# The exponential's bias by two sums over neighbouring columns of one tile

## The chip, the cores and the metric

The kernel runs on one core of a Trainium2 chip. The metric is the device time of one execution in microseconds (us): the median of several runs, beside the time of one execution that was recorded by the hardware profiler.

## What is computed

Three layers follow one another: attention with random features (the part that the change is in), a dense layer with a sigmoid-gated unit, and a layer of eight experts of which each token takes one.

```python
def phi(x):                                   # x: q or k, scaled
    proj = np.einsum('bhsd,md->bhsm', x, omega)
    sq = np.sum(x * x, axis=-1, keepdims=True) / 2.0
    h = proj - sq
    h = h - np.max(h, axis=-1, keepdims=True)
    return np.exp(h) / np.sqrt(m)
q_p, k_p = (phi(q_s), phi(k_s))
kv = np.einsum('bhsm,bhsd->bhmd', k_p, v)
z = np.sum(k_p, axis=2)
num = np.einsum('bhsm,bhmd->bhsd', q_p, kv)
den = np.einsum('bhsm,bhm->bhs', q_p, z)[..., None] + 1e-06
out = num / den
...
g = h * (1.0 / (1.0 + np.exp(-1.702 * h)))    # h = x @ w_in
x = g @ w_out
...
ye = np.maximum(xe @ w1[e], 0.0) @ w2[e]      # e: the token's expert
```

Four batches, eight heads, 576 positions, head dimension 64 and 128 features make 2304 tokens of width 512.

## The kernel before

The tokens lie in 18 tiles of 128, each with all eight heads. The attention part goes over two sequences of tiles, k and q, with the k tiles five ahead (`LEAD`). First come the five k tiles alone. Then a loop over t does, as far as they exist: normalise q tile t-2 (`norm`), project k tile t+5 (`proj`), its bias and exponentials (`expo`), transpose the exponentials of q tile t-1 (`qtr`), add a k tile to the sums over keys (`ksums`), project q tile t, its bias and exponentials, then the numerator of q tile t-1 (`num`) and the transposed output of t-2 (`xtr`). From t = 13 on there are no k tiles left, and only q tiles are worked on. The order in the code is the order on every engine (`manual_schedule`); each engine runs its own instructions in order and waits on semaphores of the others.

For one tile the steps that matter are these. GpSimd squares the raw input (L219). TensorE sums the squares with a matmul against a column of `-0.5/sqrt(D)` (L227) into a corner of a PSUM bank; VectorE copies these sums for one k and one q tile into the SBUF tile `nsq` (L232, `sqkeep`). TensorE projects the tile into two PSUM banks `pj` (L256). VectorE takes the negated maximum over the 128 features of each of the eight heads, one instruction a bank (L263), into the SBUF tile `nm`, and then forms the bias in two operations of 128x8 elements: `nm - nsq` and then `nm + nsq` (L265, L266). The pair gives the same value as the negated maximum up to rounding: what is subtracted is the rounded `max + nsq`, as in the reference. ScalarE then takes the exponentials, eight instructions a tile, each with one column of `nm` as its bias (L269).

All PSUM banks of this part come from one pool of six (`work_bank`), so a step takes the banks that an earlier step of the sequence gave up: the numerator of one tile, with the norm sums in a corner of its first bank, takes the banks of the k projection, which are free when the k exponentials have read them.

Beside this, the dense layer's weights are converted, a chunk at a time: ScalarE takes an absolute value (L139), VectorE does four steps (L117, L118, L120, L122, handed out one by one by `cpop` behind `expo`), ScalarE rounds (L164) and GpSimd subtracts (L172, `clow`, and L179 for the activations' low halves). GpSimd's tensor_tensor instructions read both inputs from SBUF.

`nm` and `nsq` have three buffers each. An `nsq` buffer serves one k and one q tile.

Of the kernel before, what the change touches and what calls it, by code (L numbers as in the profile page):

```python
# [10 lines left out]
F32 = mybir.dt.float32  # L11
# [4 lines left out]
ALU = mybir.AluOpType  # L16
AX = mybir.AxisListType
# [53 lines left out]
def fused_kernel(ctx: ExitStack, tc: tile.TileContext, qT, kT, vt, omT, w_in, w_out, w_gate, w_gateT, w1, w2, consts, out):  # L71
    nc = tc.nc
# [115 lines left out]
    sp = sctx.enter_context(tc.tile_pool(name="atts", bufs=1, side="left"))  # L188
# [21 lines left out]
    sqs, nsq = {}, {}  # L210
# [16 lines left out]
                    nc.tensor.matmul(p[c:c + 64, 8 * i + j:8 * i + 8:4], s[:, j, c:c + 64], half, start=True, stop=True)  # L227

    def sqkeep(p, tiles):
        o = sp.tile([128, 2, 2, 4], F32, name="nsq", tag="nsq", bufs=3)  # L230
        n = len(tiles)
        nc.vector.tensor_copy(out=o[:, 0:n].rearrange("p a b c -> p (a b c)"), in_=p[:, 0:8 * n])  # L232
        for i, a in enumerate(tiles):
            nsq[a] = o[:, i]

    def sqfirst(tiles):
        p = work_bank("sq").rearrange("p a b -> p (a b)")
        sqsum(p, tiles)
        sqkeep(p, tiles)


    pj, phi = {}, {}
    kvps, kvsb = {}, {}

    def work_bank(name, w=128):
        return wkp.tile([128, 4, w], F32, name=name, tag="wk", bufs=6)
# [10 lines left out]

    def expo(kind, t):
        e = phi[kind, t] = (qp if kind == "q" else kp).tile([128, H, M], F32, name="phi" + kind, tag="phi" + kind, bufs=3)
        ps2, ns = pj.pop((kind, t)), nsq.pop((kind, t))  # L260
        nm = sp.tile([128, 2, 4], F32, name="nm", tag="nm", bufs=3)
        for g, p in enumerate(ps2):
            nc.vector.tensor_reduce(out=nm[:, g], in_=p, axis=AX.X, op=ALU.max, negate=True)  # L263

        nc.vector.tensor_tensor(out=nm, in0=nm, in1=ns, op=ALU.subtract)  # L265
        nc.vector.tensor_tensor(out=nm, in0=nm, in1=ns, op=ALU.add)  # L266
        for j in range(4):
            for g, p in enumerate(ps2):
                nc.scalar.activation(e[:, 2 * j + g], p[:, j], AF.Exp, bias=nm[:, g, j:j + 1])  # L269
# [62 lines left out]
    def norm(t):  # L332
        if t in rows:
            sqkeep(rows.pop(t), tiles(t + 2))
        dn = qp.tile([128, H], F32, name="dn", tag="dn", bufs=2)
        x = xns[t] = qp.tile([128, DM], F32, name="xn", tag="xn", bufs=2)
        for g, p in enumerate(nus[t]):
            nc.vector.tensor_scalar(out=dn[:, 4 * g:4 * g + 4], in0=p[:, :, D], scalar1=1e-6 * M, scalar2=None, op0=ALU.add)
        nc.vector.reciprocal(out=dn, in_=dn)
        for g, p in enumerate(nus.pop(t)):  # L340
            nc.vector.tensor_tensor(out=x[:, 256 * g:256 * g + 256].rearrange("p (h d) -> p h d", h=4), in0=p[:, :, 0:D],
                                    in1=bc(dn[:, 4 * g:4 * g + 4], D, 2), op=ALU.mult)
# [26 lines left out]
    for i in range(WARM):  # L369
        p = work_bank("wm")  # L370
# [54 lines left out]
    for t in range(LEAD):  # L425
        proj("k", t)
        sqfirst([("k", t)])
        expo("k", t)
        if t >= 1:
            ksums(t - 1)  # L430
        advance()
        if t >= LEAD - 2:
            cload(1)
    for t in range(NT):
# [5 lines left out]
        if k < NT:  # L440
            proj("k", k)
            expo("k", k)
            advance()
# [5 lines left out]
        if k == NT:  # L449
            kctx.close()  # L450
            xa = ctx.enter_context(tc.tile_pool(name="xa", bufs=1, side="right"))
            php = ctx.enter_context(tc.tile_pool(name="ph", bufs=1, space=PSUM, side="right"))
        proj("q", t)
        expo("q", t)
        cstore()
        cabs(1)
# [280 lines left out]
    for n in range(len(steps) + 1):  # L737
        if n < len(steps):
            b, f = steps[n]
# [51 lines left out]
            if (b, f) == (0, HF):  # L791
                assert cnext[4] == len(order)
                for i in range(2):
                    wg.append(keep.tile([128, 4, DM], F32, name=f"wg{i}", tag=f"wg{i}", bufs=1))
                    nc.sync.dma_start(out=wg[i].rearrange("p e d -> p (e d)"),
                                      in_=w_gate[4 * i:4 * i + 4].rearrange("(o e) d -> o (e d)", o=1).to_broadcast([128, 4 * DM]))
# [23 lines left out]
        if n < len(steps):  # L820
# [9 lines left out]
            if wg and (b, f) not in pfirst:  # L830
                room = BUDGET[b]
                while pend and room > 0:
                    a = pend.pop(0)
# [301 lines left out]
```

## Time and profile before

| what | value |
|---|---|
| runs: median (lowest to highest) | 839.61 us (837.99 to 841.62), 3 runs |
| the profiled execution | 842.98 us |
| its span, first to last instruction | 841.1 us |
| TensorE busy | 793.1 us, 94% |
| VectorE busy | 490.0 us, 58% |
| ScalarE busy | 372.5 us, 44% |
| GpSimd busy | 127.0 us, 15% |

Times in the profile are in us from the start of the span, those of single instructions partly in ns. PE is TensorE (PEld its weight loads), DVE VectorE, ACT ScalarE, POOL GpSimd, SP the queue that issues the transfers. L265 is line 265 of the kernel. A row such as `nm<-nm,nsq 128x8` says what is written from what, with the partitions and elements. In brackets stands how long the engine was idle before the instruction and what released it; where several things were waited for, the one that came last by the profile is named, and it can have been another. "issue" is idle time for which the profile shows no wait. The granted clock (PEclk) is 1.00 at TensorE's full 2.4 GHz and 0.50 at 1.2 GHz. A busy TensorE is not necessarily one at its peak, since matmuls are pipelined.

### The profile page before, as it was taken

Reading aid. Unit: us, or ns where it says so; the run is one execution under the profiler, and the core shown is the slowest. Engines: PE = TensorE matmul, PEld = TensorE weight load, DVE = VectorE, ACT = ScalarE, POOL = GpSimd, SP = SyncE. Lnnn points to the kernel's source line nnn. Section 1 sums busy time; section 2 is a strip of 40 time slices with the busy share of each in tenths; the row PEclk is TensorE's granted clock in tenths of the full one; section 3 lists DMA queues with packets and bytes.
Section 4 is the critical chain, followed back from the end, with each engine's and each line's share of the span. In section 5 each row is a group of like instructions: output and inputs, shape, how many; then the busy total and the mean of one; then the engine's idle time right before and its main releaser. Section 6 shows DMA issues by size and latency. Waiting matters only on the chain.

```text
span 841.1 us, 17414 instructions
## 1 busy us (share of the span) xinstructions
PE 793.1 (94%) x6833; PEld 704.6 (84%) x6833; DVE 490.0 (58%) x1170; ACT 372.5 (44%) x873; POOL 127.0 (15%) x131
## 2 busy tenths in 40 slices
PE   9888888977999999999999999999999999999994
PEld 7777777755878888888888988998999999999993
DVE  3566565666986631786631775473488565556551
ACT  4666666774554433122222222222444655555551
POOL 2332222220000001010001001200014312201111
PEclk9988888998999999999999999999999999999998
DMA  8633443335888646444333644796227656555101
GB/s 219 189 101 115 116 115 102 114 101 175 289 303 272 190 157 217 130 149 149 95 94 88 183 128 122 223 344 206 88 66 293 210 204 223 182 182 185 30 29 32
DMA packets 68410, 134.74 MB, mean 160 GB/s; under 512 B 24800, under 2 KB 24928, under 8 KB 63968
## 3 DMA queue, kind: packets, MB, share of 16 engines
q1 hardware_dynamic: 65088, 124.04, 46.2%
q0 software_dynamic: 3072, 9.44, 3.8%
q8 instruction: 56, 0.92, 0.5%
q14 instruction: 34, 0.28, 0.1%
q10 hardware_dynamic: 160, 0.07, 0.0%
HBM read 118.84 MB, written 18.87 MB: 164 GB/s over the span
## 4 chain that ended last, share of the span: by engine, by line
PE 58%; issue 25%; POOL 7%; DVE 6%; ACT 2%; DMA 1%; POOLq 0%; SPq 0%; ACTq 0%; DVEq 0%
PE py L511 7%; PE py L512 7%; PE py L514 7%; PE ph L485 7%; PE ph L486 7%; PE ph L487 7%; PE pj L256 4%; POOL out L894 2%; PE tr L312 2%; PE kv L286 2%; POOL yg L679 2%; PE nu L227 2%; PE nu L330 2%; DVE nm L263 1%; POOL sq L219 1%
## 5 line engine op out<-in xcount | busy, mean ns | idle before, releaser
L500 ACT ACTIVATE gh<-ph 128x512 fp32r<-128x512 f32 (+1 forms) x80 | 44.5, 556 | 233.2 <-PE ph L487 233.2
L502 DVE TENSOR_TENSOR gl<-sg,gh 128x512 fp32r<-128x512 f32 (+1 forms) x80 | 51.1, 639 | 161.1 <-ACT sg L501 160.9
L487 PE MATMUL ph<-xh,l 128*128 128x512 f32 (+1 forms) x320 | 118.0, 369 | 1.6 <-DMA l<-lod 1.6
L485 PE MATMUL ph<-xh,win 128*128 128x512 f32 (+1 forms) x320 | 118.8, 371 | 0.0
L486 PE MATMUL ph<-xl,win 128*128 128x512 f32 (+1 forms) x320 | 117.8, 368 | 0.3 <-DVE xl L179 0.3
L511 PE MATMUL py<-wo,gh 128*128 128x512 f32 x288 | 113.6, 394 | 4.6 <-ACT big L348 4.6
L512 PE MATMUL py<-l,gh 128*128 128x512 f32 x288 | 113.5, 394 | 0.0
L546 DVE CUSTOM_DVE_ANT_0 junk<-ysb,wg 128x512 f32<-128x512 f32 x120 | 87.0, 725 | 3.1
L514 PE MATMUL py<-wo,gl 128*128 128x512 f32 x288 | 79.3, 393 | 0.0
L179 POOL TENSOR_TENSOR xl<-big,xh 128x512 fp32r<-128x512 f32 (+1 forms) x20 | 24.2, 1210 | 328.5 <-PE py L512 168.4
L851 PE MATMUL ph<-yhl,wh 128*128 128x288 f32 x256 | 71.8, 303 | 0.0
L867 PE MATMUL oT<-gh,wh 128*128 128x288 f32 x256 | 71.2, 301 | 0.0
L852 PE MATMUL ph<-yhl,wh 128*128 128x288 f32 x256 | 69.9, 295 | 0.0
L868 PE MATMUL oT<-gh,l 128*128 128x288 f32 x256 | 69.3, 294 | 0.0
L487 PEld LDWEIGHTS ph<-xh,l 128*128 128x128 f32 x320 | 60.0, 188 | 9.5 <-DMA l<-lod 2.0
L486 PEld LDWEIGHTS ph<-xl,win 128*128 128x128 f32 x320 | 60.1, 188 | 9.1 <-DVE xl L179 0.7
L511 PEld LDWEIGHTS py<-wo,gh 128*128 128x128 f32 x288 | 54.5, 189 | 15.4 <-ACT big L348 4.9
L485 PEld LDWEIGHTS ph<-xh,win 128*128 128x128 f32 x320 | 60.2, 188 | 8.6
L263 DVE TENSOR_REDUCE nm<-pj 128x4 f32<-128x512 f32 x72 | 46.3, 684 | 34.0 <-PE pj L256 31.2
L514 PEld LDWEIGHTS py<-wo,gl 128*128 128x128 f32 x288 | 54.7, 190 | 11.9
L512 PEld LDWEIGHTS py<-l,gh 128*128 128x128 f32 x288 | 54.7, 190 | 10.4
L179 DVE TENSOR_TENSOR l<-f,wh 128x512 fp32r<-128x512 f32 x64 | 46.3, 751 | 27.3 <-ACT wh L178 27.1
(187 smaller groups left out, 1492.5 us busy)
## 6 DMA issues: line engine op xcount, KB each, us to landing
l<-lod SPq DMA_DIRECT2D x160, 256.0 KB, 3.1
f<-w SPq DMA_DIRECT2D x20, 1024.0 KB, 6.1
e<-w SPq DMA_DIRECT2D x16, 1024.0 KB, 5.3
st<-w_in SPq DMA_DIRECT2D x16, 512.0 KB, 5.0
st<-w_out SPq DMA_DIRECT2D x16, 512.0 KB, 5.0
lod<-l SPq DMA_DIRECT2D x32, 256.0 KB, 2.1
yd<-ysb SPq DMA_DIRECT2D x22, 256.0 KB, 2.5
raw<-kT SPq DMA_DIRECT2D x18, 256.0 KB, 2.8
```

Source lines behind the costliest of these rows:

```text
L179: eng.tensor_tensor(out=lo, in0=src, in1=hi.bitcast(F32), op=ALU.subtract)
L485: nc.tensor.matmul(p, wh[:, c], xh, start=k == 0, stop=False)
L486: nc.tensor.matmul(p, wh[:, c], xl, start=False, stop=False)
L487: nc.tensor.matmul(p, wl[:, c], xh, start=False, stop=k == KC - 1)
L511: nc.tensor.matmul(p, gh[:, c], wh, start=(b, f) in pfirst, stop=False)
L512: nc.tensor.matmul(p, gh[:, c], wl, start=False, stop=False)
L514: nc.tensor.matmul(p, gl[:, j * 128:(j + 1) * 128], wh, start=False, stop=(b, f) in plast)
L546: nc.vector.tensor_tensor_reduce(out=junk, in0=ysb[b][j], in1=wg[e // 4][:, e % 4], scale=1.0, scalar=0.0, op0=ALU.mult, op1=ALU.add, accu ...
L851: nc.tensor.matmul(p, wh[:, w], yh[:, k], start=k == 0, stop=False)
L852: nc.tensor.matmul(p, wh[:, w], yl[:, k], start=False, stop=False)
L867: nc.tensor.matmul(p, wh[:, w], hh, start=f == 0, stop=False)
L868: nc.tensor.matmul(p, wl[:, w], hh, start=False, stop=False)
```

## The change

The tile `nsq` gets three columns for each of the eight heads: the maximum (column 0), the sum of squares (column 1), and a scratch value (column 2). The copy of the sums of squares writes column 1. The maxima are no longer negated and go to column 0. The first of the two operations becomes a negated sum over columns 0 and 1, written to column 2; the second a sum over columns 1 and 2, written to `nm`. The values are the same. Line numbers below these lines go up by one.

```diff
--- before.py
+++ after.py
@@ -227,9 +227,10 @@
                     nc.tensor.matmul(p[c:c + 64, 8 * i + j:8 * i + 8:4], s[:, j, c:c + 64], half, start=True, stop=True)
 
     def sqkeep(p, tiles):
-        o = sp.tile([128, 2, 2, 4], F32, name="nsq", tag="nsq", bufs=3)
+
+        o = sp.tile([128, 2, 8, 3], F32, name="nsq", tag="nsq", bufs=3)
         n = len(tiles)
-        nc.vector.tensor_copy(out=o[:, 0:n].rearrange("p a b c -> p (a b c)"), in_=p[:, 0:8 * n])
+        nc.vector.tensor_copy(out=o[:, 0:n, :, 1].rearrange("p a b -> p (a b)"), in_=p[:, 0:8 * n])
         for i, a in enumerate(tiles):
             nsq[a] = o[:, i]
 
@@ -257,13 +258,13 @@
 
     def expo(kind, t):
         e = phi[kind, t] = (qp if kind == "q" else kp).tile([128, H, M], F32, name="phi" + kind, tag="phi" + kind, bufs=3)
-        ps2, ns = pj.pop((kind, t)), nsq.pop((kind, t))
+        ps2, o = pj.pop((kind, t)), nsq.pop((kind, t))
         nm = sp.tile([128, 2, 4], F32, name="nm", tag="nm", bufs=3)
         for g, p in enumerate(ps2):
-            nc.vector.tensor_reduce(out=nm[:, g], in_=p, axis=AX.X, op=ALU.max, negate=True)
-
-        nc.vector.tensor_tensor(out=nm, in0=nm, in1=ns, op=ALU.subtract)
-        nc.vector.tensor_tensor(out=nm, in0=nm, in1=ns, op=ALU.add)
+            nc.vector.tensor_reduce(out=o[:, 4 * g:4 * g + 4, 0], in_=p, axis=AX.X, op=ALU.max)
+
+        nc.vector.tensor_reduce(out=o[:, :, 2], in_=o[:, :, 0:2], axis=AX.X, op=ALU.add, negate=True)
+        nc.vector.tensor_reduce(out=nm.rearrange("p a b -> p (a b)"), in_=o[:, :, 1:3], axis=AX.X, op=ALU.add)
         for j in range(4):
             for g, p in enumerate(ps2):
                 nc.scalar.activation(e[:, 2 * j + g], p[:, j], AF.Exp, bias=nm[:, g, j:j + 1])
```

The sequence of instructions stays on every engine; what changes on VectorE is the operations and what they wait for. Here are VectorE's rows in the attention loop for one k tile, before (in brackets the engine whose semaphore is waited for; `nm` is the bias, `nsq` the sums of squares, `pj` the projection, `cf` a weight chunk, `dn` and `xn` the normalised output):

```order
L341 TENSOR_TENSOR xn<-nu,dn 128x256
L263 TENSOR_REDUCE nm<-pj 128x4 [waits PE_49,Activation_49]
L263 TENSOR_REDUCE nm<-pj 128x4 [waits PE_49]
L265 TENSOR_TENSOR nm<-nm,nsq 128x8 [waits DVE_49]
L266 TENSOR_TENSOR nm<-nm,nsq 128x8 [waits DVE_49]
L122 SCALAR_TENSOR_TENSOR cf<-st_111,cf 128x512
```

and in the changed kernel at the same place:

```order
L342 TENSOR_TENSOR xn<-nu,dn 128x256
L264 TENSOR_REDUCE nsq<-pj 128x4 [waits PE_49] x2
L266 TENSOR_REDUCE nsq<-nsq 128x8 [waits DVE_49]
L267 TENSOR_REDUCE nm<-nsq 128x8 [waits DVE_49,Activation_49]
L122 SCALAR_TENSOR_TENSOR cf<-st_111,cf 128x512
```

The wait on ScalarE, for the exponentials that last read this buffer of `nm`, stands at the second sum now instead of the first maximum. The rows before and behind are the same instructions as before.

## Rows read from the trace of the kernel before

**Rows 1.** Busy time by stretch: stretch; us; busy us by engine; granted clock; DMA; GB/s.
```profile
40.00:152.00 112.00, 95.54 (x1950) 83.42 (x1952) 70.79 (x180) 71.29 (x226) 29.33 (x27) 0.83 0.40 111
```

**Rows 2.** Operations on the tile nm: count; ns min/median/max; first and last start.
```profile
L265 DVE TENSOR_TENSOR nm<-nm,nsq x36: 166/168/1283, 9.6 to 182.3; 128x8 f32<-128x8 f32 x36
```

**Rows 3.** Order of time, 73.9 to 81.4 us: start, us, engine, line, operation, idle before.
```profile
73.99 1.27 POOL L172 TENSOR_TENSOR l<-cf,win 128x512 fp32r<-128x512 f32 x1 [4.11 <-ACT win L164]
74.01 1.26 DVE L265 TENSOR_TENSOR nm<-nm,nsq 128x8 f32<-128x8 f32 x1
75.21 1.04 POOL L219 TENSOR_TENSOR sq<-raw 128x512 f32<-128x512 f32 x1
75.31 0.96 DVE L266 TENSOR_TENSOR nm<-nm,nsq 128x8 f32<-128x8 f32 x1
76.20 0.41 DVE L118 TENSOR_SCALAR cf<-cf 128x512 int32<-128x512 int32 x1
76.37 2.18 ACT L269 ACTIVATE phik<-pj,nm 128x128 f32<-128x128 f32 x8 [2.46 <-DVE nm L266]
...
79.55 2.04 POOL L219 TENSOR_TENSOR sq<-raw 128x512 f32<-128x512 f32 x2 [3.29 <-PE nu L227]
81.27 0.17 DVE L232 COPY nsq<-nu 128x16 f32<-128x16 f32 x1 [2.46 <-PE nu L330]
```

**Rows 4.** Order of time, TensorE: the norm sums at L227, 39 to 109 us.
```profile
39.92 1.10 PE L227 MATMUL nu<-half,sq 128*64 128x2 f32 x32 [1.19 <-issue]
...
48.48 1.10 PE L227 MATMUL nu<-half,sq 128*64 128x2 f32 x32 [0.74 <-issue]
...
57.65 1.66 PE L227 MATMUL nu<-half,sq 128*64 128x2 f32 x32 [1.69 <-POOL sq L219]
...
68.06 1.10 PE L227 MATMUL nu<-half,sq 128*64 128x2 f32 x32 [0.45 <-issue]
...
78.39 1.88 PE L227 MATMUL nu<-half,sq 128*64 128x2 f32 x32 [2.66 <-issue]
...
89.03 1.10 PE L227 MATMUL nu<-half,sq 128*64 128x2 f32 x32 [0.69 <-issue]
...
98.47 1.54 PE L227 MATMUL nu<-half,sq 128*64 128x2 f32 x32 [2.08 <-issue]
...
108.77 1.10 PE L227 MATMUL nu<-half,sq 128*64 128x2 f32 x32 [0.33 <-issue]
```

**Rows 5.** Busy time by stretch: the microsecond from 41 us.
```profile
41.00:42.00 1.00, 1.00 (x23) 1.00 (x23) 0.07 (x1) 1.00 (x6) 1.00 (x2) 0.50 0.08 23
```

**Rows 6.** Busy time by stretch, VectorE on tile nsq (L265, L266): busy; clock; DMA.
```profile
26.00:27.20 1.20, 1.05 (x2) 1.00 0.77 280
53.90:55.55 1.65, 1.31 (x2) 1.00 0.73 230
69.00:70.15 1.15, 1.01 (x2) 1.00 1.01 353
73.90:76.30 2.40, 2.23 (x2) 1.00 0.78 212
94.50:96.40 1.90, 1.65 (x2) 1.00 0.81 199
...
158.00:159.50 1.50, 1.16 (x2) 1.00 0.48 171
169.80:171.80 2.00, 1.84 (x2) 1.00 0.00 0
182.20:184.22 2.02, 1.83 (x2) 1.00 0.00 0
```

**Rows 7.** Operations on the tile om, at 614 us.
```profile
L953 DVE TENSOR_TENSOR om<-oh,start x1: 301/301/301, 614.5 to 614.5; 128x144 f32<-128x144 bf16 x1
L954 DVE TENSOR_REDUCE pgt<-om x1: 303/303/303, 614.8 to 614.8; 128x18 f32<-128x144 f32 x1
```

**Rows 8.** Groups of instructions from 40 to 152 us: the maxima.
```profile
L263 DVE TENSOR_REDUCE nm<-pj 128x4 f32<-128x512 f32 x45 | 29.0, 684 | 22.5 <-PE pj L256 22.5
```

## Prediction

> **What bounds the kernel now.** I read the busy time by stretch first, then the operations on the bias tile, the order of time around one slow tile, and last TensorE's idleness along the attention part. The first two show where a change in this code can act: L265 runs from 9.6 to 182.3 us of the span [rows 2], so what is saved there moves the rest forward as it stands; and from 40 to 152 us TensorE's granted clock is 0.83 on average [rows 1].
>
> The two operations that the change removes should be equal small pieces of work, 128x8 elements each, and most are: the median of L265 is 168 ns, but the longest of the 36 took 1283 [rows 2], and L266 is like it. Time order shows why. At 74.01 us L265 starts beside GpSimd's subtract (L172, at 73.99 for 1.27 us) and lasts 1.26 us; L266 starts at 75.31 beside GpSimd's square (at 75.21 for 1.04 us) and lasts 0.96 us: each ends as the GpSimd instruction ends [rows 3]. The small copy at 81.27, whose input lies in PSUM, takes its usual 0.17 us inside the two squares of 79.55 to 81.59 [rows 3]. So a VectorE operation with two SBUF inputs waits for a GpSimd tensor_tensor that is running; one that reads PSUM alone does not.
>
> This wait is on the path. ScalarE's eight exponentials of the k tile start only behind L266 (76.37, for 2.18 us [rows 3]), and TensorE's next step (the norm sums, L227, and the numerator) needs the PSUM bank that the seventh of them frees: it starts at 78.39, after 2.66 us of idleness [rows 4]. I call an interval from one start of L227 to the next *heavy* where GpSimd's L172 falls on the k tile's bias (every second one: a weight chunk is converted over two tiles), else *light*. TensorE idles 1.69, 2.66 and 2.08 us at the end of the first three heavy intervals, and 0.74, 0.45, 0.69 and 0.33 us at the end of light ones [rows 4].
>
> After long idleness TensorE is slow. The 32 norm sums take 1.10 us behind gaps of 0.33 to 0.74, and 1.66, 1.88 and 1.54 us behind the long ones [rows 4]. Behind the gap of 1.19 at 39.92 too the clock fell: from 41 to 42 us it is 0.50, the 1.2 GHz level [rows 4, 5]. So a late bias is paid twice, as idleness and as a light interval at half clock.
>
> **The change, part by part.** *What goes.* Per tile (36 tiles) L265 and L266, with whatever wait each has. Rows 6 give the two together where they met GpSimd; 2 x 0.168 = 0.34 us of it is work [rows 2, 6].
> (a) Heavy k tiles: 1.31 - 0.34 = 0.97, then 1.89 and 1.31 us [rows 6], and two later ones (115 and 136 us) like the second: 8.0 us. Each is smaller than the TensorE gap behind it (1.69, 2.66, 2.08 [rows 4]), so all of it comes off the path: 8.0.
> (b) The q-only tiles at the end (from 152 us): 0.82, 1.50 and 1.49 us [rows 6]. There is no other tile to work on there: projection, maxima, bias, exponentials and transposes follow one another. I take the first two whole. In the third the chain also runs through the conversion step behind L266, which has two SBUF inputs and would meet the same GpSimd pair. Between 0 and 1.49 I take 1.2, because an operation that waited slipped in between two GpSimd instructions (L265 ended at 75.27, the square had begun at 75.21 [rows 3]). Together 3.5.
> (c) The start: 1.05 - 0.34 = 0.7 at 26 us [rows 6], bounded by 0 if the loads set the pace there; taken as 0.7.
> (d) Four q tiles among the k tiles, the costliest being of the kind of the 0.67 us at 69 us [rows 6]. Their exponentials have until the transposes, and the normalisation behind them waits for the numerator anyhow; 0.4 for all, between 0 and 4 x 0.67 = 2.7.
>
> *What comes.* Two tensor_reduce of 128x16 to 128x8 per tile. The trace has no such size; the nearest pair is a tensor_tensor on 128x144 at 301 ns and, right behind it, a tensor_reduce of 128x144 into 18 groups at 303 ns [rows 7]: groups cost nothing to speak of. Eight elements more than now are 8/144 of what of the 303 ns grows with size, at most 17 ns. Between 0 and 17 ns an operation, on some 24 tiles of the path (18 k, the last q), the far end is 0.8 us; I take 0.3. The Trainium skill speaks against the change here: "VectorE: DVE Perf Modes", section "Rules for kernel authors", calls tensor_reduce the slowest VectorE operation, to be restructured on a hot path. Its one element a cycle at 0.96 GHz makes the eight elements 8 ns, an estimate: 0.4 us on those tiles in place of my 0.3. By the rows of 301 and 303 ns the reduce is no slower than what it replaces.
>
> *What is only rearranged.* The maxima lose their sign flip and write every third element, as does the copy; both still read PSUM. The wait for the exponentials of three tiles back moves from the first maximum to the second sum, which is later and so can only be over sooner. I cost these at nothing: VectorE waits 22.5 us for projections before the 45 maxima from 40 to 152 us [rows 8]; without that cover, 10 ns more on each of 72 maxima would be 0.7 us.
>
> *What is late next.* TensorE then waits for maxima, two short sums and seven exponentials. The gaps become 1.69 - 0.97 = 0.72, 2.66 - 1.89 = 0.77 and 2.08 - 1.31 = 0.77 us. They lie by 0.74, after which the clock stayed, and below 1.19, after which it fell.
>
> (e) The clock. Heavy intervals without the wait are (57.65 - 48.48) - 0.97 = 8.20, 10.33 - 1.89 = 8.44 and 9.44 - 1.31 = 8.13 us; the light ones at half clock are 10.41, 10.64 and 10.30 [rows 4]. A light interval at full clock should then be about 8.3, so a stretch at half clock that vanishes gives 2.1 us. Five of them follow heavy tiles: 0 if none vanishes, 10.5 for all. With gaps so near 0.74 I take three: 6.3.
>
> Sum: 8.0 + 3.5 + 0.7 + 0.4 - 0.3 + 6.3 = 18.6 us. The profiled execution took 842.98 us (1.88 more than its span) and becomes 824.4. It lies 3.37 us above the median of the runs (839.61), so the forecast for the median is **821.0 us**.
>
> **The rivals.**
> *A, the clock keeps falling.* The waits go, but gaps of 0.7 us, now at the end of every interval, bring half clock as often as before: 12.3 us of gain, 827.3 us. For it: one gap of 1.19 was enough. Against: four gaps of 0.33 to 0.74 passed [rows 4].
> *B, the clock stays up* in all five: 12.3 + 10.5, so 816.8 us. The same rows speak for it.
> *C, the wait is inherited.* Behind L266 stands one step of the weight conversion (L118, at 76.20 for 0.41 [rows 3]). It now comes up while GpSimd still works. If it is held to the end of the square (76.25), VectorE is free at 76.66 instead of 76.61: the k exponentials are early all the same, and lost are (d), the 1.2 of (b) and 0.05 in five tiles: 1.9 us, 822.9 us. The Trainium skill, "SBUF — State Buffer", section "Who interferes with whom", lists tensor_scalar in its two-port mode among what contends with GpSimd, so by it L117 and L118 could be held like the two-input steps.
> *D, the change doesn't do what it says.* The sums read SBUF, and the copy at 81.27 shows only that a PSUM input escapes [rows 3]. If one SBUF input waits as well, all stays: 839.61 + 0.3 = 839.9 us. The same section of the Trainium skill says that tensor_reduce never contends on trn2; no run here shows it yet.
> *E, slower.* From 1.19 us of idleness in every interval on, half clock would be the rule: heavy intervals grow by 2.1 each (5 x 2.1 - 8.0 = +2.5), the five q-only tiles, now at 1.00 [rows 6], likewise (10.5 - 3.5 = +7.0), less (c) and (d), 1.1, and with the 0.3: 848.3 us. Against it: behind a light interval at half clock the gap is small (0.45, 0.69, 0.33 [rows 4]), so a slow TensorE closes its own gaps.
>
> **How the numbers follow.** Forecast 0.43, A 0.21, B 0.17, C 0.10, D 0.06, E 0.03. A measurement of this kernel can tell about 0.5% (4.2 us) from no change. Forecast, A, B and C are all faster by more: 0.91; D is no change: 0.06; E is slower: 0.03. The range reaches down to B with 2.1 more of (d) and the 1.6 us by which a run lay below the median: 813. Up it reaches to A without (c), without the 1.2 of (b), and with the 2 us by which a run lay above: 831.
>
> **What would show it.** In the profile after, both sums should last about 0.17 us in every tile, beside GpSimd too; if their longest is above 0.5 us, D holds. TensorE's idleness before L227 stays below 1.2 us, and the granted clock from 40 us to the end of the k tiles rises from 0.83 to about 0.93; at 0.83 it is A, at 1.00 B. The stretches behind the attention part keep their lengths. The prediction is wrong if the attention part shortens by under 8 us or by over 27.

## The result and the profile after

The changed kernel takes 817.61 us in the median of four runs (813.85 to 817.84) where the kernel before, on the same chip, takes 838.80 (836.17 to 841.62): a ratio of 0.9736, with a 95% interval from 0.9693 to 0.9780. The forecast was 821.0 in a range of 813 to 831; rival B, that the clock stays up behind all five heavy tiles, gave 816.8. The measurement lies at B.

| | before | after |
|---|---|---|
| the profiled execution | 842.98 us | 817.50 us |
| its span | 841.1 us | 815.7 us |
| TensorE's granted clock, mean of the span | 0.969 | 0.990 |

**The two sums.** The tile view of `nsq` in the changed kernel shows (count; ns min/median/max; first and last start):

```profile
L266 DVE TENSOR_REDUCE nsq<-nsq x36: 169/170/171, 9.6 to 159.7; 128x8 f32<-128x16 f32 x36
L267 DVE TENSOR_REDUCE nm<-nsq x36: 169/170/171, 9.8 to 160.0; 128x8 f32<-128x16 f32 x36
```

Where [rows 2] had a longest of 1283 ns, and the second operation one of 1191,

```profile
L266 DVE TENSOR_TENSOR nm<-nm,nsq x36: 166/166/1191, 10.0 to 183.0; 128x8 f32<-128x8 f32 x36
```

the longest of the 72 is now 171. By the medians one sum costs 2 to 4 ns more than the operation it replaces.

**TensorE's gaps and its clock.** TensorE's norm sums of the changed kernel in order of time (start, us, engine, line, operation, in brackets the idleness before), the counterpart of [rows 4]:

```profile
39.09 1.10 PE L227 MATMUL nu<-half,sq 128*64 128x2 f32 x32 [1.19 <-issue]
...
47.14 1.10 PE L227 MATMUL nu<-half,sq 128*64 128x2 f32 x32 [0.23 <-issue]
...
55.25 1.10 PE L227 MATMUL nu<-half,sq 128*64 128x2 f32 x32 [0.72 <-POOL sq L219]
...
63.69 1.10 PE L227 MATMUL nu<-half,sq 128*64 128x2 f32 x32 [0.77 <-issue]
...
71.85 1.10 PE L227 MATMUL nu<-half,sq 128*64 128x2 f32 x32 [0.77 <-POOL sq L219]
...
80.28 1.10 PE L227 MATMUL nu<-half,sq 128*64 128x2 f32 x32 [0.77 <-issue]
...
88.45 1.10 PE L227 MATMUL nu<-half,sq 128*64 128x2 f32 x32 [0.78 <-POOL sq L219]
```

and by stretch (stretch; us; busy us by engine with instructions; granted clock; DMA; GB/s):

```profile
41.00:44.00 3.00, 3.00 (x43) 2.55 (x40) 1.82 (x6) 1.85 (x7) 1.15 (x2) 0.50 0.00 0
45.00:150.00 105.00, 93.36 (x2173) 78.80 (x2169) 77.28 (x205) 82.76 (x258) 34.52 (x31) 1.00 0.45 132
```

The gaps of 1.69, 2.66 and 2.08 us at the end of the first three heavy intervals became 0.72, 0.77 and 0.78 (at 55.25, 71.85 and 88.45), as worked out. The norm sums take 1.10 us behind every one of them. In this execution half clock is left in one place of the k tiles, behind the gap of 1.19 at 39 us, which no heavy tile makes and which was there before [rows 4, 5]. From 45 to 150 us the granted clock is 1.00, the 2.4 GHz level; before, it was 0.83 from 40 to 152 us [rows 1].

It is not so in every execution. A second profiled one of the same kernel (`change_again`, experiment 6) has a gap of 0.93 us at 104 us, as this one has at 105.04; there the numerator behind it takes 1.92 us, here 1.16:

```profile
104.24 1.10 PE L227 MATMUL nu<-half,sq 128*64 128x2 f32 x32 [0.93 <-POOL sq L219]
105.16 1.92 PE L331 MATMUL nu<-kvsb,qTs 128*64 128x65 f32 x32
```

Its clock is 0.66 from 106 to 110 us, and that interval takes 9.40 us instead of 8.67.

**The wait has not gone, it has moved.** The tile view of a weight chunk `cf` in the kernel before, the three conversion steps that VectorE runs behind the bias:

```profile
L117 DVE TENSOR_SCALAR cf<-cf x32: 413/422/429, 35.7 to 294.3; 128x512 f32<-128x512 f32 x32
L118 DVE TENSOR_SCALAR cf<-cf x32: 412/427/429, 37.7 to 294.7; 128x512 int32<-128x512 int32 x32
L120 DVE SCALAR_TENSOR_TENSOR cf<-st,cf x32: 678/691/815, 40.4 to 295.2; 128x512 int32<-128x512 int32 x32
```

and in the changed kernel:

```profile
L117 DVE TENSOR_SCALAR cf<-cf x32: 416/421/1135, 34.8 to 269.3; 128x512 f32<-128x512 f32 x32
L118 DVE TENSOR_SCALAR cf<-cf x32: 415/428/1246, 36.9 to 269.8; 128x512 int32<-128x512 int32 x32
L120 DVE SCALAR_TENSOR_TENSOR cf<-st,cf x32: 680/693/1427, 39.6 to 270.3; 128x512 int32<-128x512 int32 x32
```

Time order around the heavy tile at 69 us of the changed kernel, the counterpart of [rows 3], shows who holds whom:

```profile
69.07 1.27 POOL L172 TENSOR_TENSOR l<-cf,win 128x512 fp32r<-128x512 f32 x1 [3.57 <-ACT win L164]
69.30 0.17 DVE L266 TENSOR_REDUCE nsq<-nsq 128x8 f32<-128x16 f32 x1
69.57 0.17 DVE L267 TENSOR_REDUCE nm<-nsq 128x8 f32<-128x16 f32 x1
69.66 0.97 DVE L118 TENSOR_SCALAR cf<-cf 128x512 int32<-128x512 int32 x1
69.83 2.18 ACT L270 ACTIVATE phik<-pj,nm 128x128 f32<-128x128 f32 x8 [0.84 <-DVE nm L267]
...
70.30 1.22 POOL L219 TENSOR_TENSOR sq<-raw 128x512 f32<-128x512 f32 x1
...
72.62 1.04 POOL L219 TENSOR_TENSOR sq<-raw 128x512 f32<-128x512 f32 x1 [1.10 <-PE nu L227]
72.73 0.17 DVE L267 TENSOR_REDUCE nm<-nsq 128x8 f32<-128x16 f32 x1
...
72.82 1.39 DVE L120 SCALAR_TENSOR_TENSOR cf<-st,cf 128x512 int32<-128x512 int32 x1
...
75.27 1.10 PE L257 MATMUL pj<-omx,raw 64*64 64x128 f32 x30 [0.39 <-DVE xn L342]
```

Both sums run inside GpSimd's L172 at their usual length, and ScalarE's exponentials start at 69.83, before L172 ends. The conversion step L118 behind them is held: 0.97 us instead of 0.43, past the end of L172 at 70.34. At 72.82 L120 is held too, 1.39 instead of 0.69. From 40 to 140 us the 19 steps of L117, L118 and L120 take 9.3 us more than at the medians of before (by the groups of instructions: 7 of L120 at a mean of 1265 ns, 6 of L118 at 924, 6 of L117 at 802). In heavy tiles this lies beside the exponentials and costs nothing. In the light interval (from 71.85) it does not: VectorE comes late to the normalisation `xn`, and TensorE waits 0.39 us for it. The chain of work that ended last, of the changed kernel from 69 to 76 us (start, us, what), passes through it:

```profile
70.05 1.10 PE pj L257 x32
71.15 1.28 DVE nsq L264 x2
...
72.90 1.31 DVE cf L120
...
74.70 0.43 DVE xn L342
...
75.27 0.73 PE pj L257 x17
```

**Where the 25.4 us between the two spans lie.** From the norm sums at 39 us (TensorE in order of time) to the numerator that follows the last stretch at half clock of before, L330 at 151.59, and the same one after, L331 at 131.12: 151.59 - 39.92 = 111.67 and 131.12 - 39.09 = 92.03, so 19.6. From there to the dense layer's first product `py` (199.67 and 175.76): 48.08 and 44.64, so 3.4. Behind it 641.4 and 639.9: 1.5. And 0.8 ahead of the first. The profiled execution of before was itself 3.4 us above the median of the three runs that were known then, the one of after lies at its median; so of the 25.4, some 22 are the change (839.61 - 817.61; with the fourth run of before, 838.80 - 817.61 = 21.2).

The 19.6 can be split by the intervals between the norm sums (L227, to 150.90 before and 130.44 after). The first interval is 0.5 us shorter. The five heavy ones took 49.6 us together and now take 40.9: 8.7, of which the waits by term (a) are 8.0. The five light ones behind them took 52.8 and now take 42.4: 10.4. No wait of the bias lies in the light ones; what they had is half clock.

### The profile page after: what moved, and what is told of

It reads as the page before. It is cut to its first block, busy times and chain, and to the rows that moved or that the text cites. A ratio compares the mean times of both kernels' runs of the same rounds, so it can differ in the third digit from the quotient of the medians.

```text
span 815.7 us, 17416 instructions
## 1 busy us (share of the span) xinstructions
PE 778.5 (95%) x6833; PEld 691.5 (85%) x6833; DVE 483.6 (59%) x1170; ACT 371.9 (46%) x873; POOL 128.8 (16%) x131
## 4 chain that ended last, share of the span: by engine, by line
PE 58%; issue 24%; DVE 9%; POOL 6%; ACT 2%; DMA 1%; POOLq 0%; ACTq 0%; SPq 0%; DVEq 0%
PE py L512 8%; PE py L513 8%; PE py L515 7%; PE ph L486 7%; PE ph L487 7%; PE ph L488 7%; PE pj L257 5%; PE kv L287 3%; POOL out L895 2%; POOL yg L680 2%; DVE nsq L264 2%; PE tr L313 2%; DVE cf L120 1%; PE nu L331 1%; POOL G L1003 1%
## 5 line engine op out<-in xcount | busy, mean ns | idle before, releaser
L264 DVE TENSOR_REDUCE nsq<-pj 128x4 f32<-128x512 f32 x72 | 46.4, 686 | 29.1 <-PE pj L257 29.1
L513 PEld LDWEIGHTS py<-l,gh 128*128 128x128 f32 x288 | 54.7, 190 | 10.4
```

The costliest lines, as they stand in the source:

```text
L513: nc.tensor.matmul(p, gh[:, c], wl, start=False, stop=False)
```

## The experiments

The theory: a GpSimd instruction on SBUF holds a VectorE operation with two SBUF inputs, the sums, each a tensor_reduce with one input, pass, and TensorE gains twice, in idleness and in clock. The rivals: that the new tile's columns or the moved wait give the gain; that the clock has no part in it; that the sums' own length is all that counts. Each kernel was run beside the kernel before on the same chip (medians of before: 838.92, 838.27 and 838.58 us in the three groups). Where an experiment adds lines, its line numbers are shifted by them.

**1. The new tile with the old operations.** All of the change but the operation:

```diff
-        nc.vector.tensor_reduce(out=o[:, :, 2], in_=o[:, :, 0:2], axis=AX.X, op=ALU.add, negate=True)
-        nc.vector.tensor_reduce(out=nm.rearrange("p a b -> p (a b)"), in_=o[:, :, 1:3], axis=AX.X, op=ALU.add)
+        nc.vector.tensor_tensor(out=o[:, :, 2], in0=o[:, :, 0], in1=o[:, :, 1], op=ALU.subtract)
+        nc.vector.tensor_tensor(out=nm.rearrange("p a b -> p (a b)"), in0=o[:, :, 2], in1=o[:, :, 1], op=ALU.add)
```

with the maxima negated as before.

> The changed kernel's tile with three columns, its strided maxima and copy and its moved semaphore waits, but the bias formed by two tensor_tensor (two SBUF inputs each) as before. Port theory (a tensor_tensor with two SBUF inputs waits for a running GpSimd tensor_tensor): the waits return, longest of either operation about 1.2 us, granted clock from 40 to 140 us back near 0.83, time as before, 837 to 842 us. Rival, the tile's layout or the moved waits made the gain: about 818 us, both operations at 0.17 us.

Measured: 831.29 us (827.95 to 833.54), ratio 0.9914 [0.9875, 0.9952]. The waits are back, as the tile view and time order show:

```profile
L266 DVE TENSOR_TENSOR nsq<-nsq x36: 170/172/1056, 9.5 to 172.9; 128x8 f32<-128x8 f32 x36
L267 DVE TENSOR_TENSOR nm<-nsq x36: 168/170/1186, 9.7 to 173.9; 128x8 f32<-128x8 f32 x36
```

```profile
71.70 0.17 DVE L266 TENSOR_TENSOR nsq<-nsq 128x8 f32<-128x8 f32 x1
71.76 1.27 POOL L172 TENSOR_TENSOR l<-cf,win 128x512 fp32r<-128x512 f32 x1 [3.93 <-ACT win L164]
71.98 1.07 DVE L267 TENSOR_TENSOR nm<-nsq 128x8 f32<-128x8 f32 x1
...
75.16 1.10 PE L227 MATMUL nu<-half,sq 128*64 128x2 f32 x32 [1.67 <-POOL sq L219]
```

So the columns don't remove the wait; the operation does. But this kernel is 7.6 us faster than before, which neither theory expected (837 to 842, or 818). Two things differ. Here the first operation, at 71.70, slips in ahead of L172, and only one of the two is held; in before, L265 began with L172 and L266 fell to the square behind it [rows 3]. The waits of the five heavy tiles come to 4.9 us instead of the 8.0 of term (a). And the clock held: behind gaps of 1.70, 1.67 and 2.01 us it stayed at 1.00 (42 to 112 us), and fell only behind the last two, of 1.84 and 1.67:

```profile
42.00:112.00 70.00, 58.13 (x1411) 49.91 (x1409) 51.83 (x134) 51.92 (x167) 23.43 (x22) 1.00 0.52 138
112.00:116.00 4.00, 4.00 (x45) 3.34 (x43) 2.01 (x6) 2.21 (x8) 0.78 (x1) 0.57 0.02 4
```

The wait shorter by 3.1 us and three stretches at half clock less, 6.3, would make 9.4 us, more than the 7.6; a stretch at half clock that before does not have (0.50 from 165 to 170 us, among the q-only tiles) goes against it. What shifted the order of the two engines by a fraction of a microsecond, the columns, the moved wait or something else, is not shown. And the length of one gap does not settle the clock.

**2. One of the two operations changed.** The first stays a tensor_tensor, the second is the sum:

```diff
-        nc.vector.tensor_reduce(out=o[:, :, 2], in_=o[:, :, 0:2], axis=AX.X, op=ALU.add, negate=True)
+        nc.vector.tensor_tensor(out=o[:, :, 2], in0=o[:, :, 0], in1=o[:, :, 1], op=ALU.subtract)
```

> Only the second operation is a tensor_reduce; the first stays a tensor_tensor. Port theory: in heavy intervals the first waits for one GpSimd instruction (about 0, 1.1, 0.5, 1.1, 1.1 us by the trace before), the second never. That is 3.8 us on the k tiles and 1.8 us on the q-only tiles above the changed kernel's 817.6, and TensorE's gaps of 1.3 to 1.9 us bring half clock back in about four light intervals, 4 x 2.1: 831 us. If the clock were no part of it: 823 us. If one reduce were enough to end the waits: 818 us.

Measured: 825.35 us, ratio 0.9817 [0.9749, 0.9885]; the four runs lie between 817.71 and 827.76. That is none of the three times expected; it lies between the 823 without the clock and the 831 with it. In one kernel, the one form waits and the other does not (tile view of `nsq`):

```profile
L266 DVE TENSOR_TENSOR nsq<-nsq x36: 170/172/1070, 9.8 to 166.7; 128x8 f32<-128x8 f32 x36
L267 DVE TENSOR_REDUCE nm<-nsq x36: 169/170/172, 10.0 to 167.4; 128x8 f32<-128x16 f32 x36
```

The gaps behind four of the heavy tiles are 1.25 to 1.82 us, behind the fifth 0.78, and in the profiled execution half clock came back behind the gaps of 1.31 (at 55.7 us) and 1.41 (at 107.7), though not behind those of 1.82 and 1.25 between them. Why its executions differ by 10 us no profile shows; that the clock falls in some and not in others would fit, and is not shown.

**3. GpSimd's subtract moved to VectorE**, in the kernel before:

```diff
-        clow(nc.gpsimd)
+        clow(nc.vector)
```

> The kernel before with its two tensor_tensor for the bias, but GpSimd's subtract of the weight conversion (L172) moved to VectorE, behind the q tile's bias, so that GpSimd's work no longer falls on the heavy k tiles. Port theory: the waits on the heavy k tiles go (8 us, and the half-clock stretches behind them, up to 10.5), some waits move to q tiles, and 0.69 us on VectorE ahead of the normalisation costs up to 0.7 in five intervals: 822 to 829 us. Rival, the operations' kind itself (tensor_reduce against tensor_tensor, whatever GpSimd does) made the gain: 839 to 843 us.

Measured: 825.03 us (822.52 to 827.66), ratio 0.9833 [0.9785, 0.9880], as expected. With the two old operations untouched, taking away the GpSimd instruction they met gives 13.9 us, although in the profiled execution half clock came once more, behind a gap of 0.93 us (0.55 from 106 to 117 us). Waits are left on q tiles, where GpSimd's squares are met (the longest L265 is 1032 ns). The subtract itself, 1.27 us on GpSimd, takes 0.68 on VectorE.

**4. The clock alone: filler work for TensorE.** In the kernel before, matmuls of a 128x128 identity into an unused part of a PSUM bank stand ahead of the norm sums, so that the bias still waits and TensorE is busy meanwhile:

```diff
+    def fill(n):
+        for i in range(n):
+            nc.tensor.matmul(spare[0], ident, ident, start=False, stop=False, skip_group_check=True)
...
+        if t >= 1 and k < NT:
+            fill(FILL)
         if t >= 1:
             num(t - 1)
```

with ten at first (the edit also makes the unused part of the bank addressable).

> The kernel before, with ten matmuls of 128x128 (identity by identity, about 1.3 us in all, into spare columns of a PSUM bank of the sums over keys, read by nobody) put on TensorE between the q projection and the norm sums of iterations 1 to 12. All waits of the bias stay; only TensorE's idleness of 2 to 2.8 us is filled to 0.7 to 1.5 us. If half clock follows the long idleness: granted clock in 40 to 152 us rises from 0.83 to 0.93 or more, 10.5 us come back in light intervals, some 3 us are lost where the filler is longer than the gap: about 831 us. If the clock does not follow from the gaps, or costs nothing: 839 to 843 us.

Measured: 843.07 us (839.70 to 845.05), ratio 1.0042 [1.0016, 1.0068]: nothing gained where about 831 was expected, but not a fair trial. The clock did rise, to 0.97 from 40 to 140 us, but ten fillers were too long, 2.50 us instead of the 1.3 reckoned with: nearly every interval took 9.2 us, heavy or light, and in two iterations at the end of a batch they waited for ScalarE's copy of the sums over keys. The row is from TensorE in order of time:

```profile
67.45 4.13 PE L300 MATMUL kv<-cst 128*128 128x128 f32 x20 [2.52 <-ACT kvsb L294]
```

So it was repaired: five fillers, and none in those two iterations.

> As fill_gaps (the kernel before, all waits of the bias kept), but five filler matmuls (1.25 us by the 2.5 us that ten took) and none in the two iterations where the filler itself had to wait for a copy of the sums over keys. If half clock follows long idleness of TensorE and costs time by itself: granted clock from 40 to 152 us at 0.93 or more instead of 0.83, heavy intervals stay near 10 us, light ones near 8.5 to 9.2 instead of 10.4: 828 to 834 us. If the clock were a symptom only, with the light intervals bound by something else: 838 to 843 us.

Measured: 829.31 us (826.68 to 830.88), ratio 0.9887 [0.9864, 0.9911], as expected. The bias still waits (tile view), and the clock is up (by stretch):

```profile
L266 DVE TENSOR_TENSOR nm<-nm,nsq x36: 166/168/1262, 8.9 to 168.2; 128x8 f32<-128x8 f32 x36
L267 DVE TENSOR_TENSOR nm<-nm,nsq x36: 166/167/1123, 9.1 to 169.5; 128x8 f32<-128x8 f32 x36
```

```profile
40.00:140.00 100.00, 94.77 (x2072) 81.82 (x2065) 67.67 (x181) 73.12 (x233) 28.76 (x27) 1.00 0.46 129
140.00:190.00 50.00, 40.69 (x488) 33.02 (x485) 31.14 (x80) 30.30 (x77) 10.98 (x14) 0.79 0.30 97
```

The kernel with fillers is 9.0 us faster (838.27 - 829.31), with useless work in the way. These 9.0 are not the clock's alone, for the fillers also shift when the bias meets GpSimd: in four of the five heavy tiles it now comes up as L172 ends and is held by the square only, and the waits come to 4.8 us instead of 8.0. And among the q-only tiles, where before had 1.00 [rows 6], half clock is new (the second row). What the clock gives is seen in the light intervals, in which no bias waits: their five take 43.7 us instead of 52.8, 9.1 less, fillers included. That is nearer to term (e) at five stretches, 10.5, than at the three of the forecast, 6.3. The heavy ones are 4.0 shorter, 3.1 of it the waits; from the last norm sums of the k tiles (134.60, and 150.90 before) to the dense layer's first product, 3.3 are lost.

**5. The sums' own length.** In the changed kernel the line of the second sum is written twice, and four times.

> The changed kernel with the second sum done twice. It costs about 0.2 us a tile (start to start). If the bias is on the path once in every interval (11 with k tiles), in the q-only tiles (5) and in part of the start (up to 5), that is 3 to 5 us: 821 to 823 us, TensorE's gaps 0.77 to about 0.98 us. If the bias had slack, 817.6.

> The changed kernel with the second sum done four times: 0.6 us a tile more, with no wait for GpSimd anywhere. On the path by the same count: 10 to 13 us, 828 to 831 us, TensorE's gaps about 1.4 us in every interval. If gaps between 0.74 and 1.19 us decide the clock, as the prediction had it, half clock returns in light intervals and adds up to 10 more: 835 to 841 us.

Measured: 822.24 us (820.95 to 823.05) with one more, 838.42 (836.16 to 839.85) with three more. One more sum adds 4.6 us, most of it as 0.2 us in nearly every interval, so these few elements are on the path there; one interval grew by 0.8, with half clock in it (0.57 from 107 to 111 us, behind a gap of 1.13). Three more add not 13.8, three times as much, but 20.8. The gaps grow from 0.77 over 0.97 to 1.22 to 1.39 us in nearly every interval, and with the last half clock is back for a part of most of them. TensorE in order of time with three more:

```profile
50.10 1.10 PE L227 MATMUL nu<-half,sq 128*64 128x2 f32 x32 [1.36 <-issue]
51.03 1.91 PE L334 MATMUL nu<-kvsb,qTs 128*64 128x65 f32 x32
```

The numerator takes 1.91 us there, and 1.16 at full clock. From 40 to 140 us the clock is 0.89. This kernel has no sum that waits for GpSimd, and is as slow as the one before. To see whether the excess is the clock's, the same kernel was given the five fillers.

> The changed kernel with the second sum done four times (as three_more_sums, 838.4 us) and with the five filler matmuls of fill_short ahead of each numerator of the attention loop. If part of the 20.8 us that three more sums cost is TensorE's clock, which falls behind the longer idleness, the filler should bring the clock from 40 to 140 us back to 0.97 or more, the intervals between the norm sums to 8.7 to 9.1 us (one_more_sum's 8.36 and 8.64 plus 0.2 for each of two more sums) from a mean of 9.4, and the time to 831 to 834 us. If the 20.8 us are the sums' own length on the path, the filler changes nothing or adds to it: 837 to 841 us.

Measured: 831.39 us (829.92 to 837.03), as expected: 7.0 us come back, and the clock is 1.00:

```profile
40.00:140.00 100.00, 93.73 (x2052) 80.97 (x2040) 81.50 (x246) 69.92 (x225) 31.70 (x27) 1.00 0.43 125
```

So of the 20.8 us 7.0 come back with the clock, in a kernel whose sums never wait for GpSimd, and the 13.8 that stay are three times the 4.6 of one sum.

**6. The inherited wait taken off the path.** In the changed kernel the second conversion step of a loop pass is handed out behind the normalisation:

```diff
         if t >= 2:
             norm(t - 2)
         else:
             sqfirst(tiles(t))
+        if t >= 1:
+            cpop(1)
...
             xtr(t - 2)
-        cpop(1)
         chigh(1)
...
     norm(NT - 2)
+    cpop(1)
     sctx.close()
```

> The changed kernel with the second of each iteration's two conversion steps moved behind the normalisation (from behind the q tile's bias), so that the step that now waits for GpSimd (L120 and L117, 1.1 to 1.4 us instead of 0.69 and 0.42) no longer stands ahead of the normalised output, for which TensorE idles 0.39 us in light intervals. If that inherited wait is on the path: 0.3 to 0.4 us in each of about six light intervals and up to 1 us in the q-only tiles, 814 to 816 us. If it is covered: 817.6.

Measured: 816.38 us (813.86 to 816.98), ratio 0.9729 [0.9711, 0.9747], between the two expectations (814 to 816, or 817.6) and too near the change to be told from it. So both were run side by side.

> The changed kernel once more, beside its variant with the second conversion step behind the normalisation, on the same chip: 817 to 818 us by all theories.

> The variant with the second conversion step behind the normalisation, beside the change on the same chip. If the 0.3 us that the conversion step costs in every light interval is on the path of the whole, five intervals give 1.5 us: 815.5 to 816.5 us where the change takes 817.6. If it is caught up again behind the attention part, both take the same within 0.5 us.

Measured: the change 817.64 us (815.17 to 819.41), as expected; the variant 814.22 (813.40 to 816.91), below the 815.5 to 816.5 expected; six runs each. TensorE's norm sums of the variant in order of time:

```profile
61.11 1.10 PE L227 MATMUL nu<-half,sq 128*64 128x2 f32 x32 [0.77 <-issue]
69.24 1.10 PE L227 MATMUL nu<-half,sq 128*64 128x2 f32 x32 [0.77 <-POOL sq L219]
77.38 1.10 PE L227 MATMUL nu<-half,sq 128*64 128x2 f32 x32 [0.77 <-issue]
```

Nearly every interval is now 8.13 or 8.14 us, light or heavy, where the change has 8.43 for light ones and 8.16 for most heavy ones. The ten intervals from the first norm sums took 118.32 - 36.65 = 81.7 us in the variant and 121.94 - 38.30 = 83.6 in the change: 2.0 us, of which 1.0 is the one interval of 9.40 us with half clock in it, and 1.7 more lie ahead of them, where the start differs between executions of any of these kernels by as much. So the inherited wait costs 1 to 3 us (the two comparisons of medians give 1.2 and 3.4; the 0.3 us in five light intervals would be 1.5), and this variant has the lowest median of the study, at 0.9712 [0.9685, 0.9740] of before, though its runs overlap with those of the change.

## Why the prediction came out as it did

- *That the wait is a GpSimd instruction holding an operation with two SBUF inputs, and that the sums escape it*: shown. The sums are 169 to 171 ns in all 72 cases, and in experiment 2 the two forms stand side by side. Rival D is out. But one SBUF input is not what frees the sums: the conversion steps L117 and L118 have one, and are held up to 1135 and 1246 ns. What the runs show to escape is the tensor_reduce, not every operation with one input. The Trainium skill, "SBUF — State Buffer", section "Who interferes with whom", states that tensor_reduce never contends with GpSimd on trn2; this trace agrees.
- *Term (a), 8.0 us, and the gaps of 0.72 to 0.77*: the gaps came out right to 0.01 us, and the five heavy intervals are 8.7 us shorter, with what (d) adds in them.
- *Term (e), 6.3 us*: this is the step that failed, by its size. I took three of five stretches, because 0.77 lies just above the longest gap after which the clock had stayed. In the profiled execution all five went, and the five light intervals are 10.4 us shorter: (e) at 10.5 and the other terms as they were give 22.8 us, and the medians differ by 22.0 (21.2 with the fourth run of before). In the second profiled execution one of the five was back in part, at 0.7 us. Rival B was the better description, for which the text had 0.17. Together (a) and (e) were put at 14.3 and B's at 18.5; measured between the norm sums at 39 us and the end of the k tiles are 19.6, 0.5 of them in the first interval.
- *The reason for that choice, a threshold between 0.74 and 1.19 us of idleness*: too simple. Gaps of 0.93 to 0.97 in nearly every interval left the clock up (one more sum), and gaps of 1.22 to 1.39 in nearly every interval brought it down for a part of most of them (three more). But a gap of 0.93 left it up in one execution of the changed kernel and not in the other, nor in experiment 3, and gaps of 1.7 to 2.0 in every second interval did not bring it down before 110 us in experiment 1, though 1.69 to 2.83 did in before each time. What decides is open; it was not tried by itself.
- *Term (b), 3.5 us*: 3.4 between these two executions. *Term (c), 0.7*: 0.8 in the two traces, but the start scatters by more than that from execution to execution, so this shows nothing. *Term (d), 0.4* can't be told apart.
- *The price of the reduces, 0.3 us*: 2 to 4 ns more each, so 0.1 to 0.2 us on the path's 24 tiles. The Trainium skill, "VectorE: DVE Perf Modes", section "Rules for kernel authors", calls tensor_reduce the slowest VectorE operation; at 128x16 elements the trace has 170 ns beside 166 to 168 for the tensor_tensor of the same result, so here the rule doesn't bear.
- *Rival C, the inherited wait*: true as a mechanism, wrong in place and price. Steps of all three kinds, L117, L118 and L120, are held, not one L118, and the cost is 0.3 us in each light interval, where VectorE's normalisation is late, not in the q tiles' exponentials. At 1 to 3 us it is of the size worked out, 1.9, but beside a clock that stays up.
- *The maxima, the copy and the moved wait, costed at nothing*: that they cost nothing stands, for experiment 1 has them all and is not slower than before. It is 7.6 us faster, which the text had no term for: with the old operations the order in which they meet GpSimd changed. In the changed kernel no sum waits, so on the bias that order has nothing to act there.
- *That the later stretches keep their lengths*: within 1.5 us of 641.

## What to carry to other kernels

A small operation whose median is short and whose longest is many times that is waiting for something the median hides: look at what the other engines run at those moments. If it is a tensor_tensor with both inputs in SBUF, held by a GpSimd instruction, rewriting it as a reduction over neighbouring columns took it out of the way here at nearly the same length, and the wait passed to the next operations that GpSimd can hold, one-input steps among them; so see to it that these have slack. And where TensorE's gaps are long enough to cost it its clock, a microsecond of idleness taken off the path can be worth twice its length (here 8.7 and 10.4 us). Filler matmuls can tell the clock's part, if the intervals are compared one by one: the fillers also shift which operations meet.

## What was not expected of the hardware

- VectorE's one-input conversion steps are held as well: L118 took up to 1246 ns beside GpSimd, and 429 at most before. GpSimd is held in return: in the changed kernel an L172 on GpSimd takes up to 1722 ns, and 1281 at most before. The same section of the Trainium skill on SBUF lists tensor_scalar among what can contend; the trace agrees.
- Useless matmuls of 1.38 us in most intervals made the kernel before 9.0 us faster, in part by shorter waits (experiment 4), and the one with three more sums 7.0 us.
- Gaps of 1.7 to 2.0 us did not always bring half clock, as told in experiment 1, and one of 0.93 us did in one execution of the changed kernel and not in another.
